# Mean and 1/std of three chunks sent round through DRAM, with their columns on partitions from the start, in a fused long-convolution and Mish-MLP kernel

## The chip, the cores and the metric

The kernel runs on one core of a Trainium2 chip. The metric is the device time of one execution in microseconds (us).

## The reference

The input q has 2048 rows of 448 columns. The kernel adds three things: q itself, a gated long convolution, and an MLP. Both branches work on the layer-normed q.

```python
x = A_q
xn = _layernorm(x, axis=-1)          # (x - mean) / sqrt(var + 1e-5), without scale and shift
return x + _A_ref(xn, A_k, A_v, A_shift_k, A_ssm_k, A_ssm_D) + _B_ref(xn, B_w1, B_b1, B_w2)
# _A_ref: kv = (causal conv of k with 4 taps) * v
#         y  = causal conv of kv with a 2048-long filter per column (by FFT) + kv * D;   result xn * y
# _B_ref: h  = xn @ w1 + b1  (448 -> 1792);  act = h * tanh(softplus(h));   result act @ w2  (1792 -> 448)
```

## The kernel before

**Layout.** The 2048 rows form 8 chunks of 256 rows. A chunk is two row groups `jj` of 128 rows with rows on partitions. The layout is [128 partitions, 16 groups, 448 columns].

**The MLP on TensorE (PE).** Each chunk has seven pairs `p` of 256 hidden units, so there are 56 pairs. Numbers are split into a high part (fp32r) and a rest (fp32r), and products are summed from three parts. A pair has a first product (`g1_mm`, L437, 22 matmuls with the columns of q on partitions: `XH`, `XL`), Mish on ScalarE (ACT; `mish`, L445), a split of the result (`ach` by ACT, `acl` by VectorE (DVE), L73 and L74), and two pairs later a second product (`g2_mm`, L462 to L464, 12 matmuls).

**The layer norm.** `ln_load` fetches the chunk's rows, `Q[c]`. `ln_parts` holds the steps: statistics on DVE (L369 to L375, ending in `ve` = var + eps), 1/std by a power on GpSimd (POOL, L378), the normed rows `xn` on POOL for chunks 1 to 6 and on DVE for chunks 0 and 7 (L382), and a copy of the last 64 columns (L386). The first product wants columns on partitions. So `ln_T` puts four PE transposes per row group (L397) into a PSUM buffer of the first product, ACT casts them to `XH` (L409) and DVE subtracts to get `XL` (L407). Mean and 1/std also serve the gate at the end, in `mv` and `rstd`.

**The convolution** has four steps and uses PSUM buffers of its own, two `pc` of two banks. First, transforms of 8 groups of the filter and of kv (`f1_mm`, L124) go to DRAM, `Dh` and `Dkv`. Then there are eight octets of frequencies: loads `ah` and `av`, a pass over H and a pass over V (`f2_mm`, L198), which ACT copies out as `hs` and `vs`, products on DVE (`prod`, L231: `ya`, `yb`, `yc`, `yd`) and an inverse pass (`i1_mm`, L241), whose result `qe` goes to `E` in DRAM. The last step loads `E` by chunk (`e_load`, L274, two halves `jj` of 64 partitions, both from POOL's queue), folds it on DVE (L280, L282), multiplies (`i2_mm`, L300) and gates (`gate`, L313 and L315).

**The outputs.** For chunks 0 to 5 the MLP's sum goes to DRAM as `ACC` and comes back for the gate: `qa_load` fetches q and ACC into one of three buffers, and `gate_out` sends the result out, all on SyncE's queue (SP). Chunks 6 and 7 stay in SBUF until the end; their MLP sums are added by `g2_evac` (L469), which also sends them out.

**The order** is set by hand. Each pair is two half steps: the even one holds the first product, the odd one Mish and the second product of the pair two back. `at(t, ...)` puts work ahead of half step t, `after(t, ...)` behind it. `H0_AT` and `OCT_AT` place the octets, `I2_AT` the four groups of two chunks of the last step. Small DVE operations wait in the list `drip` and are taken one by one by `dv()` between others; `dv(len(drip))` empties it. Every engine works its own list in order, and so does each DMA queue.

Of the kernel before, what the change touches and what calls it, by code (L numbers as in the profile page):

```python
# [7 lines left out]
F32 = mybir.dt.float32  # L8
# [9 lines left out]
NP = NF // 2  # L18
# [6 lines left out]
H_HEAD = 1  # L25
H_AT = {2: 4, 3: 8, 0: 12, 4: 16, 5: 20, 6: 26, 7: 32}
KV_AT = (24, 29, 34, 39, 44, 50, 55, 60)
H0_AT = 63
OCT_AT = (65, 3)
I2_AT = {98: (6, 7), 102: (0, 1), 106: (2, 3), 111: (4, 5)}  # L30
LATE = 2
WARM = 4
WARM_N = 448


@with_exitstack
def tile_kernel(ctx: ExitStack, tc, q, k, v, sk, hT, sD, w1, b1, w2, c_f1, c_g, c_gi, c_i2, out):
    nc = tc.nc
    V = nc.vector

# [14 lines left out]
    Dkv = dp.tile([NO * 16, 32, D], F32, name="Dkv")  # L55
    E = dp.tile([64, NJ * 4, D], F32, name="E")
    ACC = dp.tile([128, NJ, D], F32, name="ACC")

    f1id = cp.tile([128, 2, 128], F32, name="f1id")
    f1, ident = f1id[:, 0], f1id[:, 1]  # L60
# [11 lines left out]
    def split(h, l, raw):  # L72
        nc.scalar.copy(h, raw)  # L73
        V.tensor_sub(l, raw, h)  # L74
# [7 lines left out]
    def dv(n=1):  # L82
        for _ in range(n):
            if drip:
                drip.pop(0)()
# [183 lines left out]
    def e_load(c):  # L269

        e = EE[c] = t3([128, 2, 2, D], "e3", 4)
        src = E.rearrange("(h k) (m j b) d -> j k m h b d", h=2, m=2, b=2)
        for jj in range(2):
            nc.gpsimd.dma_start(e[64 * jj:64 * jj + 64].rearrange("p h b d -> p h (b d)"),  # L274
                              src[2 * c + jj].rearrange("k m h b d -> (k m) h (b d)"))

    def fold(c):
# [70 lines left out]
        split(w2h[:, 2 * p:2 * p + 2], w2l[:, 2 * p:2 * p + 2], RW.pop(("2", p)))  # L348


    XS, XN = {}, {}

    def ln_load(c, eng=None):
        Q[c] = mp.tile([128, 2, D], F32, name="qt", tag="qt", bufs=3)
        if c:
            nc.sync.dma_start(Q[c], q[:, 2 * c:2 * c + 2])
        else:
            for jj in range(2):
                nc.sync.dma_start(Q[c][:, jj], q[:, jj])

    def ln_parts(c):
        st = mp.tile([128, 2, 6], F32, name="bst", bufs=2)
        ve = mp.tile([128, 2], F32, name="ve", bufs=2)
        xn = mp.tile([128, 2, D + 64], F32, name="xn", tag="xn", bufs=1)
        XN[c] = xn
        eng = nc.gpsimd if 0 < c < NCHUNK - 1 else V

        def stats(jj):
            V.bn_stats(st[:, jj], Q[c][:, jj])  # L369

        def aggr(jj):
            V.bn_aggr(mv[:, 2 * c + jj], st[:, jj])

        def eps(a, b):
            V.tensor_scalar(ve[:, a:b], mv[:, 2 * c + a:2 * c + b, 1], EPS, None, op0=ALU.add)  # L375

        def power(a, b):
            nc.gpsimd.tensor_tensor(rstd[:, 2 * c + a:2 * c + b], ve[:, a:b], mhalf[:, a:b], op=ALU.pow)  # L378

        def norm(jj):  # L380
            j = 2 * c + jj
            eng.tensor_scalar(xn[:, jj, :D], Q[c][:, jj], mv[:, j, 0:1], rstd[:, j:j + 1],  # L382
                              op0=ALU.subtract, op1=ALU.mult)

        def tail(a, b):
            eng.tensor_copy(xn[:, a:b, D:], xn[:, a:b, D - 64:D])  # L386

        return stats, aggr, eps, power, norm, tail

    def ln_stats(c):  # L390
        stats, aggr, eps, power, norm, tail = ln_parts(c)
        drip.extend([lambda: stats(0), lambda: stats(1), lambda: aggr(0), lambda: aggr(1), lambda: eps(0, 2),
                     lambda: [f(*a) for f, *a in ((power, 0, 2), (norm, 0), (norm, 1), (tail, 0, 2))]])

    def transposes(c, jj, p):
        for kt in range(4):
# [79 lines left out]
    def mlp_slot(s):  # L476
        i, half = divmod(s, 2)
        n = len(pairs)
        j = i - G2_LAG
        if half == 0:  # L480
            if i < n:
                c, p = pairs[i]
                if c + 1 < NCHUNK:
                    if p == 0:
                        ln_load(c + 1)
                    if p == (2 if c else 3):
                        ln_stats(c + 1)
                    if c == 0:
                        dv(len(drip))
                    if p == NP - 1:  # L490
                        ln_T(c + 1, 1)
                g1_mm(i)
        else:
            if i < n:
                c, p = pairs[i]
                if p == NP - 2 and c + 1 < NCHUNK:
                    ln_T(c + 1, 0)
                mish(i)
            if 0 <= j < n - 1:
# [179 lines left out]
```

## Time and profile before

| | |
|---|---|
| time, median of 3 runs (lowest, highest) | 378.37 us (377.31, 380.5) |
| the profiled execution's own time | 377.21 us |
| its span, first to last instruction | 375.3 us |
| granted clock of PE, mean | 0.996 |
| DMA | 82.11 MB, mean 219 GB/s |

In rows of engine work a timeline gives start (us from the span's start), duration, engine, line and operation with output and inputs, and in brackets the idle time before it with what ended it. A row of a group (lines) gives the count, busy us in all, mean ns of one, then the engine's idle time before them. PEld is PE's weight load, which overlaps the matmuls; a matmul's row lasts longer than its distance to the next, since matmuls are pipelined, so what one costs PE is read from start to start. A row of DMA issues gives KB of one and the median us from issue to landing.

### The profile page before, as it was taken

The numbers are of one execution on the slowest core, as the hardware profiler recorded it, in microseconds if no ns is written. First come the engines' busy times: TensorE is split into PE (matmuls) and PEld (weight loads), VectorE is DVE, ScalarE is ACT, GpSimd is POOL, SyncE is SP. The second block draws the span as 40 slices with busy tenths as digits, with TensorE's granted clock in tenths as the row PEclk, the third lists the DMA queues.
The fourth block names the chain that finished last, engine by engine and source line by source line (L and its number), as shares of the span: only waits on it lengthen the run. The fifth ranks groups of instructions, "written<-read, shape, count | busy, mean of one in ns | idle before, by whom it ended". The sixth has DMA issues, their size and how long they took to land.

```text
span 375.3 us, 7470 instructions
## 1 busy us (share of the span) xinstructions
PE 364.6 (97%) x3128; PEld 293.0 (78%) x3128; DVE 277.2 (74%) x370; ACT 158.7 (42%) x265; POOL 52.3 (14%) x49
## 2 busy tenths in 40 slices
PE   8999999999999999999999999999999999999994
PEld 2788888878888988988886666666666799688973
DVE  3899748999999999996534746744754915799593
ACT  2785642434424423333433755554755243213210
POOL 2107000700051003300023000140000005220000
PEclk9999999999999999999999999999999999999998
DMA  8899968749488427604885587868480778999466
GB/s 307 308 308 342 388 227 236 205 109 284 121 279 239 100 51 246 196 3 103 255 264 184 207 273 244 274 221 277 153 296 33 253 291 190 224 190 274 155 192 249
DMA packets 32564, 82.11 MB, mean 219 GB/s; under 512 B 2962, under 2 KB 18195, under 8 KB 32531
## 3 DMA queue, kind: packets, MB, share of 16 engines
q1 hardware_dynamic: 22130, 51.69, 41.4%
q10 hardware_dynamic: 9120, 22.61, 20.1%
q0 software_dynamic: 1280, 7.34, 8.7%
q8 instruction: 24, 0.39, 0.4%
q14 instruction: 10, 0.07, 0.1%
HBM read 53.19 MB, written 28.44 MB: 218 GB/s over the span
## 4 chain that ended last, share of the span: by engine, by line
PE 63%; DMA 14%; DVE 13%; issue 4%; ACT 4%; POOL 1%; ACTq 0%; DVEq 0%; SPq 0%; POOLq 0%
PE pg L437 26%; PE pg L462 8%; PE pg L463 7%; PE pg L464 7%; PE pc L198 7%; DMA out_dram<-q 4%; PE pc L124 3%; PE pc L241 3%; DMA a<-ACC 3%; DMA e<-E 2%; ACT a L445 2%; DMA Dkv<-st 1%; PE pg L397 1%; DMA av<-Dkv 1%; DVE acl L74 1%
## 5 line engine op out<-in xcount | busy, mean ns | idle before, releaser
L445 ACT ACTIVATE a<-pg,b1t 128x256 f32<-128x256 f32 x112 | 47.0, 472 | 119.7 <-PE pg L437 101.2
L437 PE MATMUL pg<-XH,w1h 128*128 128x256 f32 x448 | 91.1, 285 | 1.2 <-ACT XH L409 0.7
L437 PEld LDWEIGHTS pg<-XH,w1h 128*128 128x128 f32 x448 | 69.6, 188 | 18.1 <-issue 15.7
L462 PE MATMUL pg<-w2h,ach 128*128 128x448 f32 x224 | 83.3, 372 | 0.2 <-DVE qt L469 0.2
L463 PE MATMUL pg<-w2l,ach 128*128 128x448 f32 x224 | 81.4, 363 | 0.6 <-DVE w2l L74 0.6
L464 PE MATMUL pg<-w2h,acl 128*128 128x448 f32 x224 | 81.4, 363 | 0.0
L74 DVE TENSOR_TENSOR acl<-a,ach 128x512 fp32r<-128x512 f32 x56 | 38.4, 686 | 47.9 <-ACT ach L73 47.7
L437 PE MATMUL pg<-XL,w1h 128*128 128x256 f32 x448 | 69.6, 277 | 0.0
L437 PEld LDWEIGHTS pg<-XL,w1h 128*128 128x128 f32 x448 | 59.4, 188 | 0.1
L437 PE MATMUL pg<-XH,w1l 128*128 128x256 f32 x336 | 56.8, 278 | 0.0
L462 PEld LDWEIGHTS pg<-w2h,ach 128*128 128x128 f32 x224 | 42.0, 187 | 12.7 <-issue 10.4
L437 PEld LDWEIGHTS pg<-XH,w1l 128*128 128x128 f32 x336 | 46.8, 188 | 0.1
L463 PEld LDWEIGHTS pg<-w2l,ach 128*128 128x128 f32 x224 | 42.1, 188 | 3.5 <-DVE w2l L74 1.1
L378 POOL TENSOR_TENSOR rstd<-ve,mhalf 128x2 f32<-128x2 f32 (+1 forms) x9 | 8.5, 944 | 258.6 <-DVE ve L375 220.3
L464 PEld LDWEIGHTS pg<-w2h,acl 128*128 128x128 f32 x224 | 42.1, 188 | 2.6
L73 ACT CAST ach<-a 128x512 fp32r<-128x512 f32 x56 | 34.7, 620 | 1.8
L382 POOL TENSOR_SCALAR xn<-qt,mv,rstd 128x448 f32<-128x448 f32 x12 | 28.3, 2361 | 0.6
L162 DVE TENSOR_TENSOR x<-x 128x896 f32<-128x896 f32 x24 | 26.7, 1113 | 0.8
L409 ACT CAST XH<-pg 128x512 fp32r<-128x512 f32 x16 | 9.4, 587 | 36.9 <-PE pg L397 36.7
L407 DVE TENSOR_TENSOR XL<-pg,XH 128x512 fp32r<-128x512 f32 x16 | 10.9, 686 | 13.7 <-ACT XH L409 13.5
L130 ACT COPY st<-pc 128x896 f32<-128x896 f32 x16 | 14.5, 909 | 15.3 <-PE pc L124 13.2
L131 DVE TENSOR_TENSOR st<-pc,st 128x896 f32<-128x896 f32 x16 | 17.4, 1087 | 3.4 <-ACT st L130 3.1
(63 smaller groups left out, 393.3 us busy)
## 6 DMA issues: line engine op xcount, KB each, us to landing
Dh<-st ACTq DMA_DIRECT2D x16, 448.0 KB, 5.4
Dkv<-st ACTq DMA_DIRECT2D x16, 448.0 KB, 5.2
ah<-Dh SPq DMA_DIRECT2D x8, 896.0 KB, 5.2
av<-Dkv SPq DMA_DIRECT2D x8, 896.0 KB, 4.9
E<-qe ACTq DMA_DIRECT2D x8, 896.0 KB, 4.6
e<-E POOLq DMA_DIRECT2D x16, 448.0 KB, 10.0
kr<-in_k_dram SPq DMA_DIRECT2D x10, 448.0 KB, 6.6
kr<-in_w_dram SPq DMA_DIRECT2D x7, 512.0 KB, 6.4
```

What stands on the lines that cost most here:

```text
L73: nc.scalar.copy(h, raw)
L74: V.tensor_sub(l, raw, h)
L130: nc.scalar.copy(st[:, 1], o)
L131: V.tensor_add(st[:, 0], e, st[:, 1])
L162: V.tensor_add(KV[g], KV[g], o)
L198: nc.tensor.matmul(p[32 * t:32 * t + 32, r, :D], g[rs, t, c], a[rs, t], start=True, stop=True, tile_position=(64 * r, 32 * t))
L382: eng.tensor_scalar(xn[:, jj, :D], Q[c][:, jj], mv[:, j, 0:1], rstd[:, j:j + 1], op0=ALU.subtract, op1=ALU.mult)
L437: nc.tensor.matmul(ps[:, n], l, r, start=n_ == 0, stop=n_ == len(mm) - 1)
L445: nc.scalar.activation(a[:, n], ps[:, n], AF.Mish, bias=b1t[:, 2 * p + n:2 * p + n + 1])
L462: nc.tensor.matmul(ps, ah[:, n, cs], w2h[:, f], start=f == 0, stop=False)
L463: nc.tensor.matmul(ps, ah[:, n, cs], w2l[:, f], start=False, stop=False)
L464: nc.tensor.matmul(ps, al[:, n, cs], w2h[:, f], start=False, stop=f == NF - 1)
```

## The change

For chunks 5 to 7 (`QT_FROM` = 5) a further input `qT` holds q's rows with columns on partitions, cut into three blocks [128, 4, 256]; the fourth 128 columns are the last 64 twice, as with the copy in the kernel before. `qT_load` fetches a block into the tile `xn`. `ln_out` writes the chunk's means and 1/std, 256 numbers each, to the DRAM tile `MR` (values of 4 bytes, two per partition), and `ln_back` reads those 512 numbers into all 128 partitions, both on POOL's queue. `ln_apply` puts four passes on DVE, two that subtract and two that multiply; `x_both` casts `XH` on ACT and subtracts `XL` on DVE. The chunk's transposes, its normed rows on POOL or DVE and their copy fall away. `Q[c]` is still loaded, for the statistics and the sums; its three buffers are now named, and the broadcast lands in the one that is free at that time.

The octets and their first H pass stand one half step later, and three of the four groups of the last step too; the last group stays. The second half `jj` of the slabs of the first group (chunks 6 and 7) is loaded from SP's queue.

```diff
-H0_AT = 63
-OCT_AT = (65, 3)
-I2_AT = {98: (6, 7), 102: (0, 1), 106: (2, 3), 111: (4, 5)}
+H0_AT = 64
+OCT_AT = (66,3)
+I2_AT = {99: (6, 7), 103: (0, 1), 107: (2, 3), 111: (4, 5)}
 LATE = 2
+QT_FROM = 5
...
+    MR = dp.tile([NCHUNK, 2, 2, 128], F32, name="MR")
...
         for jj in range(2):
-            nc.gpsimd.dma_start(e[64 * jj:64 * jj + 64].rearrange("p h b d -> p h (b d)"),
+            (nc.sync if jj and c in I2_AT[min(I2_AT)] else nc.gpsimd).dma_start(e[64 * jj:64 * jj + 64].rearrange("p h b d -> p h (b d)"),
...
-    XS, XN = {}, {}
+    XS, XN, MB = {}, {}, {}
+    QB = [mp.tile([128, 2, D], F32, name="qt%d" % n, bufs=1) for n in range(3)]
 
     def ln_load(c, eng=None):
-        Q[c] = mp.tile([128, 2, D], F32, name="qt", tag="qt", bufs=3)
+        Q[c] = QB[c % 3]
...
-        xn = mp.tile([128, 2, D + 64], F32, name="xn", tag="xn", bufs=1)
-        XN[c] = xn
-        eng = nc.gpsimd if 0 < c < NCHUNK - 1 else V
+        if c < QT_FROM:
+            XN[c] = xn = mp.tile([128, 2, D + 64], F32, name="xn", tag="xn", bufs=1)
+        eng = nc.gpsimd if c else V
...
-                     lambda: [f(*a) for f, *a in ((power, 0, 2), (norm, 0), (norm, 1), (tail, 0, 2))]])
+                     lambda: [f(*a) for f, *a in ((power, 0, 2),) + (((norm, 0), (norm, 1), (tail, 0, 2)) if c < QT_FROM else ())]])
+
+    def ln_out(c):
+        for w, t in enumerate((mv[:, 2 * c:2 * c + 2, 0], rstd[:, 2 * c:2 * c + 2])):
+            nc.gpsimd.dma_start(MR[c, w].rearrange("j p -> p j"), t)
+
+    def ln_back(c):
+        MB[c] = QB[(c + 1) % 3].rearrange("p a b -> p (a b)")[:, :2 * CH].rearrange("p (a b) -> p a b", a=2)
+        nc.gpsimd.dma_start(MB[c], MR[c].rearrange("w j p -> (w j p)").partition_broadcast(128))
+
+    def qT_load(c):
+        XN[c] = mp.tile([128, 4, CH], F32, name="xn", tag="xn", bufs=1)
+        nc.sync.dma_start(XN[c], qT[c - QT_FROM])
+
+    def ln_apply(c):
+        x, mb = XN[c], MB.pop(c)
+        for op, w in ((V.tensor_sub, 0), (V.tensor_mul, 1)):
+            for kt in range(0, 4, 2):
+                drip.append(lambda op=op, w=w, kt=kt: op(x[:, kt:kt + 2], x[:, kt:kt + 2], mb[:, w:w + 1].to_broadcast([128, 2, CH])))
+
+    def x_both(c):
+        dv(len(drip))
+        x_tiles(c)
+        split(*XS[c], XN.pop(c))
...
-                    if p == NP - 1:
+                    if p == NP - 1 and c + 1 < QT_FROM:
                         ln_T(c + 1, 1)
...
-                if p == NP - 2 and c + 1 < NCHUNK:
+                if p == NP - 2 and c + 1 < QT_FROM:
                     ln_T(c + 1, 0)
...
+    for c in range(QT_FROM, NCHUNK):
+        t = 2 * NP * (c - 1)
+        after(t + 6, lambda: dv(len(drip)))
+        at(t + 7, qT_load, c)
+        at(t + 7, ln_out, c)
+        at(t + 7, ln_back, c)
+        after(t + 8, ln_apply, c)
+        after(t + 10, lambda: dv(len(drip)))
+        after(t + 11, x_both, c)
```

Three places show the new order. The first is PE in the octet stage, ahead of chunk 5's first product, in the kernel before (`ah` and `av` are octet 1's passes; rows of `pg` with `ach` are the second product, with `XH` the first):

```order
L198 MATMUL pc<-ah,g 32x448 x16
L397 MATMUL pg_2265<-f1id,xn 128x128 x4
L462 MATMUL pg_2053<-w2h,ach 128x448
...
L464 MATMUL pg_2057<-w2h,acl 128x448
L198 MATMUL pc<-av,g 32x448 x16
L397 MATMUL pg_2319<-f1id,xn 128x128 x4
L437 MATMUL pg_2326<-XH,w1h 128x256 x3
```

The two rows of transposes (`f1id,xn`) are gone in the change, here and in chunks 6 and 7; nothing takes their place on PE.

The second is chunk 7: POOL from the power to the first slabs of the last step, in the change,

```order
L381 TENSOR_TENSOR rstd<-ve,mhalf 128x2
L401 DMA MR<-mv 128x2x1
L401 DMA MR<-rstd 128x2x1
L406 DMA qt_95<-MR 128x512
L276 DMA e_3489<-E 64x2x896
L276 DMA e_3492<-E 64x2x896
L276 DMA e_3522<-E 64x2x896 x2
```

and DVE from octet 7's products to the folds of the first group, before and then in the change (`yc` and `yd` are products, `z` and below is the gate, not shown):

```order
L375 TENSOR_SCALAR ve<-mv 128x2
L74 TENSOR_TENSOR acl<-a,ach 128x512
L382 TENSOR_SCALAR xn<-qt,mv,rstd 128x448 x2
L386 COPY xn<-xn 128x2x64
L407 TENSOR_TENSOR XL<-pg_3520,XH 128x4x128
L74 TENSOR_TENSOR acl<-a,ach 128x512
L280 TENSOR_TENSOR ex<-e_3479 128x896
L282 TENSOR_TENSOR e_3479<-e_3479 128x896
```

```order
L378 TENSOR_SCALAR ve<-mv 128x2
L233 TENSOR_TENSOR yd<-vs,hs 128x896
L233 TENSOR_TENSOR yc<-yc,yd 128x896
L76 TENSOR_TENSOR acl<-a,ach 128x512 x2
L416 TENSOR_TENSOR xn<-xn,qt_95 128x512 x4
L76 TENSOR_TENSOR acl<-a,ach 128x512
L76 TENSOR_TENSOR XL<-xn,XH 128x1024
L282 TENSOR_TENSOR ex<-e_3489 128x896
L284 TENSOR_TENSOR e_3489<-e_3489 128x896
```

On POOL the two writes of `MR` and the broadcast (into `qt_95`) stand behind the power, and of chunks 6 and 7 (`e_3489`, `e_3492`) one half each is left. On DVE `ve` stands ahead of the last products instead of behind them, and two products and two `acl` lie between it and the passes over `xn`.

The third is PE at the second group of the last step (`pc<-ex` and `pc<-e`), before and then in the change:

```order
L464 MATMUL pg_3348<-w2h,acl 128x448
L300 MATMUL pc<-ex,i_3450 32x448 x2
...
L437 MATMUL pg_3751<-XH,w1h 128x256 x3
...
L462 MATMUL pg_3795<-w2h,ach 128x448
```

```order
L492 MATMUL pg_3326<-w2h,acl 128x448
L465 MATMUL pg_3708<-XH,w1h 128x256 x3
...
L302 MATMUL pc<-ex,i_3457 32x448 x2
...
L490 MATMUL pg_3756<-w2h,ach 128x448
```

The group stands behind the first product of that pair instead of ahead of it. On SP, the q and ACC loads of the second and third chunk of the last step now stand behind the two `e` halves.

More of the change, by code (lines that the diff above doesn't have):

```diff
@@ L36, in tile_kernel @@
 @with_exitstack
-def tile_kernel(ctx: ExitStack, tc, q, k, v, sk, hT, sD, w1, b1, w2, c_f1, c_g, c_gi, c_i2, out):
+def tile_kernel(ctx: ExitStack, tc, q, qT, k, v, sk, hT, sD, w1, b1, w2, c_f1, c_g, c_gi, c_i2, out):
     nc = tc.nc
@@ L660 @@
     lay = lambda x: x.reshape(32, 2, 2, 16, D).transpose(2, 1, 0, 3, 4).reshape(128, NJ, D)
+    qT = lay(a["A_q"][0])[:, 2 * QT_FROM:].transpose(2, 1, 0)
+    qT = np.concatenate([qT, qT[384:]]).reshape(4, 128, NCHUNK - QT_FROM, CH).transpose(2, 1, 0, 3)
     kpad = np.pad(a["A_k"][0], ((4, 0), (0, 0)))
     arrs = dict(
-        q=lay(a["A_q"][0]), k=np.concatenate([lay(kpad[:S])[:, :, :][:, :4], lay(a["A_k"][0])], axis=1),
+        q=lay(a["A_q"][0]), qT=qT, k=np.concatenate([lay(kpad[:S])[:, :, :][:, :4], lay(a["A_k"][0])], axis=1),
         v=lay(a["A_v"][0]), sk=a["A_shift_k"].T, hT=lay(a["A_ssm_k"].T), sD=a["A_ssm_D"][None],
```

## Prediction

> **What bounds the kernel now.** I read the busy times first, then the stages, the waits, and last the chain that ended last. The first row is from the page; the others are the table by stage (window, length, busy time of each engine, granted clock, DMA share, GB/s).
>
> ```profile
> PE 364.6 (97%) x3128; PEld 293.0 (78%) x3128; DVE 277.2 (74%) x370; ACT 158.7 (42%) x265; POOL 52.3 (14%) x49
> 178.40:292.50 114.10, 112.92 (x1222) 79.31 (x1221) 64.02 (x76) 60.82 (x92) 11.62 (x8) 1.00 0.68 220
> 320.70:334.10 13.40, 12.78 (x101) 9.90 (x100) 12.82 (x17) 2.92 (x6) 2.34 (x4) 1.00 1.02 225
> 334.10:370.10 36.00, 35.98 (x291) 29.99 (x290) 28.88 (x41) 7.30 (x15) 2.33 (x4) 1.00 0.75 215
> ```
>
> PE is busy at full clock from the start to 370.1. In the octet stage (178 to 292) DVE works 64 us of 114, so there it has room; from 320.7 on it has little. What PE still loses shows in the waits (us in total, times, longest):
>
> ```profile
> PEld pc L300 <- DVE e L282: 1.8, 2, 1.0
> PEld pc L300 <- DVE ex L280: 1.2, 1, 1.2
> PEld pc L198 <- ACT hs L209: 1.5, 2, 0.8
> PEld pc L241 <- DVE yc L231: 1.2, 1, 1.2
> PE pc L198 <- DMA av<-Dkv: 0.3, 1, 0.3
> ```
>
> Small, but of the size of what is at stake. The chain in order of time (start, us, what) tells what sets the very end, and the last matmul stands below it:
>
> ```profile
> 338.96 9.42 DMA out_dram<-q
> 348.79 5.90 DMA a<-ACC
> 356.77 6.11 DMA out_dram<-q
> 363.28 4.94 DMA a<-ACC
> 368.31 0.69 DVE q L315
> 370.85 0.53 DVE qt L469
> ```
> ```profile
> 369.72 0.36 PE L464 MATMUL pg<-w2h,acl 128*128 128x448 f32 x1
> ```
>
> The tail is not PE. Chunks 0 to 5 share three gate buffers, so each load of q and ACC for the next chunk waits on SP's queue until an earlier chunk's out slab has landed. This string starts with chunk 0's gate and ends with chunk 5's; DVE evacuates the last sums only behind it, at 370.85. PE's last matmul ends at 370.08, so PE alone could end some 0.7 us earlier and no more.
>
> **Transposes.** The octet stage shows one chunk's pair (chunk 5):
>
> ```profile
> 200.60 0.66 PE L397 MATMUL pg<-f1id,xn 128*128 128x128 f32 x4
> 201.01 0.45 PE L462 MATMUL pg<-w2h,ach 128*128 128x448 f32 x1
> 204.13 1.79 PE L198 MATMUL pc<-av,g 64*32 64x448 f32 x32 [0.46 <-ACT hs L209]
> 205.85 0.66 PE L397 MATMUL pg<-f1id,xn 128*128 128x128 f32 x4
> 206.26 0.60 PE L437 MATMUL pg<-XH,w1h 128*128 128x256 f32 x3
> ```
>
> Four transposes hold PE from 200.60 to 201.01, 0.41 us by starts; six such groups go: **-2.4**. Their first half also queues an XH cast on ACT ahead of the hs copies, so the V pass at 204.13 waited 0.46; the same shape stands in chunk 6. In the change one XH cast from SBUF needs no PE result and stands ahead of hs only if xn is late: **-0.9** (bounds 0 and the 1.5 of the wait row).
>
> **The round trip that replaces them.** Per chunk: POOL's power, two MR issues, one broadcast issue, two landings in a row; then four subtract or multiply passes of 128x512 on DVE, one XH cast and one XL of 128x1024.
>
> ```profile
> L378 POOL TENSOR_TENSOR rstd<-ve,mhalf 128x2 f32<-128x2 f32 x7 | 7.3, 1046 | 253.2 <-DVE ve L375 220.3 <-DMA x<-in_v_dram 32.9
> L274 POOL DMA_DIRECT2D e<-E x16 | 9.6, 608 | 22.5 <-DVE acl L74 9.8 <-DVE ex L280 7.6 <-ACT ach L73 3.8
> DMA to landing us min/median/max: 5.0/10.0/15.2
> i<-in_c_i_dram SPq DMA_DIRECT2D x1, 32.0 KB, 2.4
> L74 DVE TENSOR_TENSOR acl<-a,ach 128x512 fp32r<-128x512 f32 x56 | 38.4, 686 | 47.9 <-ACT ach L73 47.7
> L330 ACT CAST w1h<-kr 128x1024 fp32r<-128x1024 f32 x6 | 6.3, 1047 | 1.1 <-DMA kr<-in_w_dram 1.1
> L209 ACT COPY hs<-pc 128x896 f32<-128x896 f32 x16 | 13.7, 909 | 3.7 <-PE pc L198 3.7
> 182.21 0.17 DVE L372 BATCH_NORM_AGGREGATE mv<-bst 128x2 f32<-128x6 f32 x1
> 209.01 1.69 PE pc L241 x32
> ```
>
> (The third row is the landing time of the e slabs, POOL's only DMAs.) Power and three issues are 1.05 + 3 x 0.61 = 2.9 us. No row shows a transfer like MR's, 256 values of 4 bytes. Below, a landing is bounded by the 32 KB constant, 2.4; above, by the quickest e slab, 5.0, since MR is far smaller and the broadcast is 256 KB against 448. Middle 3.7: 2.9 + 7.4 = **10.3 us** (7.7 to 12.9). With the e slabs' median of 10.0, eight of them queued, it is 22.9.
>
> What covers it: in chunk 7, `ve` is forced after half step 90, and chunk 7's first matmul stands in half step 98. Between lie an estimated 1.4 of half step 90, octet 7's inverse pass of 1.69, and seven products of 2.5 (first and second products; rows 299.85 to 302.46 and 318.16 to 320.66 below): 20.6 us. DVE and ACT then need 4 x 0.69 for the passes (an estimate from acl, the same size), 0.69 for an acl, 1.05 for XH and some 1.2 for XL, 5.6 in all: **15.0** are left. In chunk 5 `ve` moves up to some 182.7, behind the row at 182.21. The first that can suffer is the V pass of octet 1 in half step 69, which needs ACT's two hs copies behind XH. Until then lie 2.2 of half step 62, six products of 2.5 and three passes of 1.7, 22.3; less 2.7 for the passes, 1.05 for XH and 1.8 for hs, 16.7. So the trip is hidden with 2 us or more to spare, and so are the 2.5 us that DVE works more per chunk, in a stage where it is 56% busy. If the trip is late, acl and the octet's products queue behind the waiting passes on DVE, hs behind XH on ACT, and PE waits for those. I allow **+0.4** for small waits (bounds 0 and the third rival).
>
> The Trainium skill, "DMA: Bandwidth & Descriptors" (Rules for kernel authors), says that a non-contiguous last dimension lowers to one descriptor per element, which MR's write is. By the Trainium skill's same page (Anatomy of one DMA) a GpSimd DMA has about 2.0 us fixed, and the trip would be an estimated 7 us; the trace's e slabs never landed under 5.0. No run here shows what 256 single elements cost.
>
> **The later half steps.** Octets start half a step later, with the same spacing; this moves work and adds none. Waits at the edges (0.3 for av; the inverse pass of octet 7 broke for yc) had too little lead, and the change gives av 2.5 us more and puts `ve` of chunk 7 among the products: **-0.7** of some 1.0 (bounds 0 and 1.0).
>
> The last step's four groups stand at half steps 99, 103, 107, 111 instead of 98, 102, 106, 111.
>
> ```profile
> 299.85 0.62 PE L437 MATMUL pg<-XH,w1h 128*128 128x256 f32 x3
> 302.46 0.36 PE L462 MATMUL pg<-w2h,ach 128*128 128x448 f32 x1
> 318.16 0.37 PE L462 MATMUL pg<-w2h,ach 128*128 128x448 f32 x1
> 320.66 0.57 PE L300 MATMUL pc<-ex,i 64*32 64x448 f32 x2
> 324.10 0.62 PE L437 MATMUL pg<-XH,w1h 128*128 128x256 f32 x3
> 334.13 0.57 PE L300 MATMUL pc<-ex,i 64*32 64x448 f32 x2
> 335.80 0.62 PE L437 MATMUL pg<-XH,w1h 128*128 128x256 f32 x3
> ```
>
> The second group feeds chunk 0's gate and starts the string of the tail. It now stands behind one more first product, 302.46 - 299.85: **+2.6**. From its start, 334.13, to the span's end are 41.2 us, and this distance stays, since it is made of landings. So the end moves by all that PE gains ahead of the second group, less 2.6; what PE gains behind it is worth 0.7 at most.
>
> The first group took 320.66 to 324.10, 3.44 us; the second, unhindered, 1.67. The 1.8 between were spent on chunk 7's e slab:
>
> ```profile
> 309.53 4.90 POOL L274 DMA_DIRECT2D e<-E  x8 [3.77 <-ACT ach L73]
> 320.93 1.09 DVE L280 TENSOR_TENSOR ex<-e 128x896 f32<-128x896 f32 x1 [1.87 <-DMA e<-E]
> q0 software_dynamic: 536, 3.15, 89.7%
> ```
>
> Its halves were third and fourth of the eight that POOL issued from 309.53 on; now they are second on POOL and second on SP. They are issued once E has landed. That last E write went out beside six prefetches of q and ACC; four of these now stand behind SP's e halves and so cannot slow it. I take the wait as gone: **-1.8**. Bounds: gone, or 2 us longer, if POOL's next slabs (3.15 MB in 16 us, so 2.3 us each) slip in between.
>
> Chunk 6's out slabs, which shared their time with the four e slabs at 335, go out ahead of the second group now. The first landing of the string, 9.42 against 6.11 for a later one, can shorten: **-0.6** (bounds 0 and the 2.7 at which PE, with 36.0 - 2.6 us left, sets the end).
>
> **Sum.** -2.4 - 0.9 + 0.4 - 0.7 + 2.6 - 1.8 - 0.6 = -3.4. The profiled execution took 377.21 with a span of 375.3; 371.9 of span give **373.8 us**. The median of the runs shown is 378.37, 1.2 above the profiled one, so this is 1.2% under the median. Differences under 1% can't be told from none in this kernel; the line for faster is 374.6.
>
> **Rivals.** *The last step keeps its wait* (25%). For: POOL's queue alone held the 16 DMA engines 89.7% busy in those 16 us (last row above), so a second queue may bring e no sooner. Then the -1.8 is missing, 375.6, up to 377.7 with the longer bound. Against: the four prefetches are out of the way and E lands earlier. The Trainium skill, "DMA: Bandwidth & Descriptors" (Issuing engines are not separate DMA queues), states this rule: transfers started on several engines run on the same 16 DMA engines and interleave, and only issue time is saved; by that, the trace's 89.7% agrees.
>
> *The tail shortens until PE sets it* (13%). Chunk 6's outs are gone and the string loses 2.7 instead of 0.6: 371.7. Against: the e slabs still run there, DMA share 0.75.
>
> *The round trip is late* (13%), the case on the other side. For: its transfers wait for one another, beside octet loads at a DMA share of 0.68, and the e row's median is 10.0. Lateness is 2.9 + 2L - 15.0 in chunk 7 and 2.9 + 2L - 16.7 in chunk 5, L being one landing. From L = 7.3 it eats the 3.4, from 8.6 the kernel is over 1% slower; at 10.0 it loses 7.9 + 6.2 = 14.1, which gives 387.9. Against: the quickest e slab took 5.0 and is larger; 10.0 belongs to a queue of eight. The Trainium skill's rule of one descriptor per element, named above, speaks for this case.
>
> **How the numbers follow.** My forecast, 373.8, has 49%; its own terms spread it from 371.5 to 375.6, about 0.35 of it under 374.6. Faster: 0.35 + 0.13 + 0.03 from the first rival = 0.51. Slower: most of the late trip, 0.12. Same: the remaining 0.37. The range leaves out the worst late trips and the best tails: 370.8 to 379.0.
>
> **What would show it.** Right: 40 transposes instead of 64; no wait of PE on xn, MR or the qt tile that holds the broadcast; passes on xn starting when acl frees DVE, not when the broadcast lands; the second group near 331 and chunk 0's out slab near 336; the first group at about 1.7 us. Wrong: DVE idle ahead of xn for over 3 us with the broadcast as its releaser, hs or XH as releasers of PE in the octet stage, chunk 7's e landing after PE's slot, or a tail longer than 41 us from the second group.

## The result, and the profile after

| | before | after |
|---|---|---|
| time, median (lowest, highest), 6 runs each | 378.12 us (377.31, 382.13) | 396.17 us (393.67, 397.79) |
| ratio, 95% interval | | 1.0493 (1.0458 to 1.0528) |
| the profiled execution's own time | 377.21 us | 395.33 us |
| its span | 375.3 us | 393.5 us |
| granted clock of PE, mean | 0.996 | 0.987 |

The change makes the kernel 4.9% slower. The span grew by 18.2 us. I had forecast 3.4 us less.

The busy times, and three stretches of the table by stage (window, length, busy time of PE, PEld, DVE, ACT and POOL, granted clock, DMA share, GB/s):

```profile
PE 369.9 (94%) x3104; PEld 292.4 (74%) x3104; DVE 282.8 (72%) x376; ACT 159.1 (40%) x262; POOL 47.2 (12%) x50
181.90:217.50 35.60, 30.59 (x297) 21.82 (x295) 13.39 (x20) 13.76 (x21) 2.93 (x4) 0.95 0.62 206
317.00:340.00 23.00, 17.29 (x112) 11.97 (x111) 12.04 (x16) 8.17 (x15) 6.55 (x11) 0.93 0.81 201
340.00:381.00 41.00, 37.14 (x294) 29.19 (x292) 31.30 (x42) 8.76 (x18) 2.38 (x4) 0.96 0.87 231
```

The 24 transposes are gone from PE's count (3128 to 3104). But where PE was busy throughout before, it now stands idle for 5.0 us of the 35.6 around chunk 5, for 5.7 us of the 23 between 317 and 340, where the last step begins, and for 3.9 us of the tail. In these three stretches the mean granted clock is also lower (0.95, 0.93, 0.96): at the end of each of three stops of PE (5.0 us up to 198.8, 4.2 up to 332.4, 3.3 up to 376.9) begin 3.4 us at a clock of 0.5. The waits name who kept whom (us in total, times, longest):

```profile
POOL qt L406 <- DMA MR<-mv: 21.6, 2, 11.0
DVE xn L416 <- DMA qt<-MR: 10.6, 2, 8.2
ACT qe L251 <- DMA E<-qe: 9.7, 1, 9.7
DVE ex L282 <- DMA e<-E: 8.7, 3, 5.0
PE pc L200 <- DMA av<-Dkv: 5.0, 1, 5.0
PE pc L302 <- DVE ex L282: 4.6, 3, 3.3
```

POOL waits for the two writes of MR before it may issue the broadcast, and DVE waits for the broadcast. Two other rows name transfers that the change didn't touch: an av load and an E write. The timeline of chunk 5's trip, on POOL and on DVE:

```profile
183.03 0.95 POOL L401 DMA_DIRECT2D MR<-mv  x1
183.99 0.74 POOL L401 DMA_DIRECT2D MR<-rstd  x1
195.77 0.58 POOL L406 DMA_DIRECT2D qt<-MR  x1 [11.04 <-DMA MR<-mv]
...
201.84 2.49 DVE L416 TENSOR_TENSOR xn<-xn,qt 128x512 f32<-128x512 f32 x4 [8.23 <-DMA qt<-MR]
```

From the first write's issue to the first pass lie 18.8 us. The issues and landings around it, for 180 to 200 us, tell both stories: first after, then the two rows of before that answer to it. The row GB/s has 40 slices of half a microsecond; a row of issues ends with the median us to landing.

```profile
GB/s 149 198 273 247 262 366 394 432 424 409 419 423 392 223 81 0 0 0 0 0 0 0 0 0 0 18 47 82 32 7 54 283 401 409 406 390 402 387 387 384
...
Dkv<-st ACTq DMA_DIRECT2D x2, 448.0 KB, 10.5
av<-Dkv SPq DMA_DIRECT2D x1, 896.0 KB, 6.8
...
qt<-MR POOLq DMA_DIRECT2D x1, 256.0 KB, 6.0
...
MR<-mv POOLq DMA_DIRECT2D x1, 1.0 KB, 12.0
MR<-rstd POOLq DMA_DIRECT2D x1, 1.0 KB, 11.2
```
```profile
av<-Dkv SPq DMA_DIRECT2D x2, 896.0 KB, 4.9
Dkv<-st ACTq DMA_DIRECT2D x2, 448.0 KB, 5.3
```

A write of 1 KB takes 12.0 us. While the two are under way the data rate is zero for 5 us (187.5 to 192.5), although a Dkv write issued before them hasn't landed: it takes 10.5 us, where such a write took 5.3. The av load reads Dkv, so it is issued late (at 191.9), and the V pass of octet 0 waits for it: PE stands for 5.0 us up to 198.8, and the pass then takes 3.2 us, 1.5 more than the H pass before it, at the clock of 0.5. At chunk 7 it is a write of E that lands late. These rows give us to landing of the eight E writes (lowest, median, highest), after and then before:

```profile
DMA to landing us min/median/max: 3.9/5.7/16.9
```
```profile
DMA to landing us min/median/max: 3.8/4.6/7.1
```

The write of 16.9 us, issued at 299.74, holds its buffer; ACT's next copy `qe` waits 9.7 us for it, so the last E write goes out at 318.5 instead of 301.7. Not all of the 16.9 us can be MR's doing: chunk 7's MR writes were issued only from 305.6 on, and eleven of this E write's sixteen completion counts had come by 307.4, late already against the 4.6 us of before; the other five came from 312.0 to 316.7, the MR writes landing at 316.9 and 317.1. With PE's broadcast in place of MR (below) the same write, beside the same prefetches, takes 8.1 us. Behind that comes the chain to the end (start, us, what):

```profile
327.37 20.77 DMA e<-E
355.37 12.58 DMA out_dram<-q
368.35 5.27 DMA a<-ACC
375.66 5.38 DMA out_dram<-q
381.48 4.90 DMA a<-ACC
388.47 0.53 DVE qt L497
```

The second group starts at 348.23 and chunk 0's out slab takes 12.58 us instead of 9.42, and the slabs are among the links.

**Where the 18.2 us lie.** Four landings in the trace cut the end of the program into pieces: the last E write, the last of the sixteen e slabs, chunk 0's out slab, the span's end (us; the differences in brackets).

| | E lands | last slab | chunk 0's out slab | end of span |
|---|---|---|---|---|
| before | 308.8 | 347.3 (38.5) | 348.4 (1.1) | 375.3 (26.9) |
| after | 323.6 | 367.4 (43.8) | 368.0 (0.5) | 393.5 (25.5) |

So E lands 14.9 us later, the slabs take 5.3 us more, and the rest takes 1.9 us less. The experiments ask for the cause of the first two.

### The profile page after: what moved, and what is told of

Read it like the earlier page. It is cut to its first block, busy times and chain, and to the rows that moved or that the text cites. A ratio compares the mean times of both kernels' runs of the same rounds, so it can differ in the third digit from the quotient of the medians.

```text
span 393.5 us, 7451 instructions
## 1 busy us (share of the span) xinstructions
PE 369.9 (94%) x3104; PEld 292.4 (74%) x3104; DVE 282.8 (72%) x376; ACT 159.1 (40%) x262; POOL 47.2 (12%) x50
## 5 line engine op out<-in xcount | busy, mean ns | idle before, releaser
L381 POOL TENSOR_TENSOR rstd<-ve,mhalf 128x2 f32<-128x2 f32 (+1 forms) x9 | 7.6, 845 | 242.5 <-DVE ve L378 238.3
L302 PE MATMUL pc<-ex,i 64*32 64x448 f32 x64 | 13.4, 658 | 8.7 <-DVE ex L282 4.6
L251 ACT COPY qe<-pc 128x896 f32<-128x896 f32 x16 | 13.8, 911 | 19.3 <-DMA E<-qe 9.7
L200 PE MATMUL pc<-av,g 64*32 64x448 f32 x256 | 16.6, 591 | 5.1 <-DMA av<-Dkv 5.0
L220 ACT COPY vs<-pc 128x896 f32<-128x896 f32 x16 | 13.8, 909 | 17.8 <-PE pc L200 16.1
```

The source lines that it names most:

```text
L200: nc.tensor.matmul(p[32 * t:32 * t + 32, r, :D], g[rs, t, c], a[rs, t], start=True, stop=True, tile_position=(64 * r, 32 * t))
L220: nc.scalar.copy(PV[o][:, c], p[:, :, :D])
L251: nc.scalar.copy(qe[:, 2 * i:2 * i + 2], p[:, :, :D])
```

## The experiments

**My theory after the result:** the writes of single 4-byte values into the same 2 KB of DRAM land slowly, and transfers of other parts that are under way land late with them; the waits on both make the loss. **Rivals:** the new half steps and SP's e halves are to blame; or the trip is merely too long for its cover, as the third rival of the prediction had it, and nothing else is disturbed. Ratios are to the kernel before on the same chip, with a 95% interval.

**The two parts apart.** First the half steps and SP's halves alone, with the transposes kept; then the layout and the trip alone.

```diff
 # the kernel before
-H0_AT = 63
-OCT_AT = (65, 3)
-I2_AT = {98: (6, 7), 102: (0, 1), 106: (2, 3), 111: (4, 5)}
+H0_AT = 64
+OCT_AT = (66,3)
+I2_AT = {99: (6, 7), 103: (0, 1), 107: (2, 3), 111: (4, 5)}
...
-            nc.gpsimd.dma_start(e[64 * jj:64 * jj + 64].rearrange("p h b d -> p h (b d)"),
+            (nc.sync if jj and c in I2_AT[min(I2_AT)] else nc.gpsimd).dma_start(e[64 * jj:64 * jj + 64].rearrange("p h b d -> p h (b d)"),
```

> The kernel before with the later half steps and the SP halves of the first slabs, transposes kept. Theory (the 4-byte writes of MR are the loss): 377.6, by the forecast's own terms +2.6 - 1.8 - 0.7 - 0.6, within 375 to 381. Rival (the later half steps and the SP halves are the loss): 388 or more, most of the 18 us.

> The change without the later half steps and with all slabs on POOL's queue. Theory (MR's writes): still slow, 391 to 400, each MR write landing 10 us or more after its issue. Rival (the later half steps): 374 to 378.

The half steps alone: 378.37 us, 1.0029 (0.9998 to 1.0059). The trip alone, with the half steps and POOL's slabs of before: 403.54 us, 1.0669 (1.0587 to 1.0752). That is more than the 391 to 400 expected. The whole loss sits in the trip, and the later half steps with SP's halves even ease it. The waits of the trip alone say how:

```profile
DVE xn L416 <- DMA qt<-MR: 28.1, 3, 13.4
PE pc L243 <- ACT vs L220: 10.7, 1, 10.7
```

The passes over `xn` wait 28.1 us for the broadcast instead of 10.6, and here they do hold up PE, by way of ACT's copy `vs`, which waits for an octet's product behind them on DVE: 10.7 us. In the change this wait of PE's is 0.2 us.

**The writes alone.** The kernel before, transposes and all, with the two MR writes added for chunks 5 to 7 and nobody reading them; `ve` is forced earlier as in the change. Beside it the same without the writes, and one that gives each value 512 bytes of its own.

```diff
 # the kernel before, and this
+    def ln_out(c):
+        for w, t in enumerate((mv[:, 2 * c:2 * c + 2, 0], rstd[:, 2 * c:2 * c + 2])):
+            nc.gpsimd.dma_start(MR[c, w].rearrange("j p -> p j"), t)
...
+        after(t + 6, lambda: dv(len(drip)))
+        at(t + 7, ln_out, c)
```
```diff
 # 512 bytes for each value
-    MR = dp.tile([NCHUNK, 2, 2, 128], F32, name="MR")
+    MR = dp.tile([NCHUNK, 2, 2, 128, 128], F32, name="MR")
...
-            nc.gpsimd.dma_start(MR[c, w].rearrange("j p -> p j"), t)
+            nc.gpsimd.dma_start(MR[c, w, :, :, 0].rearrange("j p -> p j"), t)
```

> The kernel before plus the two MR writes of chunks 5 to 7 (ve forced at the same half step), which nothing reads; transposes kept, no broadcast. Theory (the writes hold up other transfers that are under way, above all Dkv and E): 384 to 392, with an E write beside them landing after 9 us or more in place of 4.6. Rival (only the passes that wait for the trip lose time): 378, no change.

> The control for the writes alone: the kernel before with only ve of chunks 5 to 7 forced at the earlier half step, no writes. Theory (all of the loss of that run is the writes): 377, no change. Rival (the earlier ve and the norm that goes with it displace DVE and POOL work): 380 to 386.

> The run with the writes alone, but each of the 512 values of a chunk goes to an address of its own 512 bytes from the next; nothing reads them. If what costs is that many small writes meet in the same 2 KB of DRAM: landings of 3 to 5 us and a time within 1% of before. If each piece costs wherever it goes: landings of 9 us or more and about 386 as before.

The writes alone: 386.21 us, 1.0227 (1.0159 to 1.0296), though no instruction waits for them. Without them 376.07 us, 1.0005 (0.9977 to 1.0034). With 512 bytes for each value 377.05 us, 1.0021 (0.9994 to 1.0048). The landings of MR (lowest, median, highest; of the crowded six only four are on record), crowded and then spread:

```profile
DMA to landing us min/median/max: 11.5/12.4/12.9
```
```profile
DMA to landing us min/median/max: 2.3/5.7/6.4
```

And those of the eight E writes in the same two kernels:

```profile
DMA to landing us min/median/max: 3.8/4.0/13.4
```
```profile
DMA to landing us min/median/max: 3.8/3.9/7.4
```

As many pieces of the same size land in half the time if each has its own 512 bytes, and the loss is gone. So the piece itself isn't what costs; the crowding is. The last E write, issued just behind the crowded MR writes of chunk 7, takes 13.4 us instead of 7.4, so E lands at 318.7; without the writes it lands at 308.5. The Trainium skill's "DMA: Bandwidth & Descriptors" (Rules for kernel authors) has one descriptor per element for such a write, which both of these kernels share, so that rule alone doesn't tell them apart. The Trainium skill's same page (Specifications) says that below 512 B the DMA engine reads, modifies and writes back; writes into the same stretch would then have to follow one another, and the landings of MR above agree with that. That it is this mechanism no run here shows.

**Whose queue.** The same writes from SP's queue instead of POOL's:

```diff
-            nc.gpsimd.dma_start(MR[c, w].rearrange("j p -> p j"), t)
+            nc.sync.dma_start(MR[c, w].rearrange("j p -> p j"), t)
```

> The kernel before with the two unread writes of 256 values of 4 bytes for chunks 5 to 7, as in the run with the writes alone, but from SP's queue instead of POOL's. Theory (the crowding of small writes in the same 2 KB of DRAM is slow, whoever issues them): they land after 9 to 13 us again, E writes or loads beside them take 9 us or more, span 382 to 387. Rival (POOL's queue is what is slow): they land in 3 to 6 us and the span is 374 to 377.

From a single run: span 392.7 us, time 394.52. MR's landings in it:

```profile
DMA to landing us min/median/max: 8.9/9.8/10.4
```

They are slow from SP too. The rival falls. The span is longer than the 382 to 387 expected; that kernel's last E write landed only at 325.9. Why that run lost more than the one from POOL's queue stays open.

**The trip cured: rows of 16 bytes.** POOL packs the two means and two 1/std of a partition into one row, and one write sends 128 rows of 16 bytes; DVE reads the broadcast with a stride.

```diff
 # the change
-    MR = dp.tile([NCHUNK, 2, 2, 128], F32, name="MR")
+    MR = dp.tile([NCHUNK, 128, 4], F32, name="MR")
...
-        for w, t in enumerate((mv[:, 2 * c:2 * c + 2, 0], rstd[:, 2 * c:2 * c + 2])):
-            nc.gpsimd.dma_start(MR[c, w].rearrange("j p -> p j"), t)
+        r = mp.tile([128, 4], F32, name="mr4", bufs=2)
+        nc.gpsimd.tensor_copy(r[:, 0:2], mv[:, 2 * c:2 * c + 2, 0])
+        nc.gpsimd.tensor_copy(r[:, 2:4], rstd[:, 2 * c:2 * c + 2])
+        nc.gpsimd.dma_start(MR[c], r)
...
```

> The change with mean and 1/std of a row put side by side on POOL, written to MR as 128 rows of 16 bytes instead of 512 single values, and read back as one piece; DVE's passes read it with a stride. Theory, if the time of a write goes with the number of its pieces: one landing near 4 us in place of 11 and 372 to 378. If a small write costs the same whatever their number: 393 to 398. Rival (the later half steps are the loss): 393 to 398 with a short landing.

378.77 us, 1.0038 (1.0000 to 1.0077). Landings of MR and broadcast together in this kernel:

```profile
DMA to landing us min/median/max: 2.3/5.4/6.1
```

These 128 rows, too, lie side by side in 2 KB and land fast: what was slow is 256 single values to a write, crowded, and not small neighbouring pieces as such. The second group starts at 331.91, where the prediction wanted it ("near 331"). The loss of 18 us is gone, and yet the kernel isn't faster than before; its 378.77 lies just above the 372 to 378 expected. The cure was then tried with POOL's queue for all slabs, and once more with the half steps of before as well:

> The rows of 16 bytes with the new half steps, but all slabs of the last step on POOL's queue again. Theory (the SP halves let the q and ACC loads of two chunks fall in among the e slabs, which lengthens the tail from the second group from 41.2 to 44 us): a tail of 41 to 42 us and 374 to 377. If the SP halves earn their place by ending the first group's wait: 378 to 381.

> The change with mean and 1/std sent as 128 rows of 16 bytes, and with the octets, the groups of the last step and the slabs' queue as in the kernel before. Theory (a trip that lands in 2 to 6 us is hidden, and the new layout then saves PE 2.4 to 3.3 us): PE reaches the second group at 331 to 332.5 and the time is 374 to 375.5, ratio 0.990 to 0.995. Rival (the trip's transfers still hold up E, as its first group waited 5.5 us in the run with the new times and POOL's slabs): the first group waits 3 us or more, second group at 334 or later, time 377 or more.

New half steps with POOL's slabs: 376.52 us, 1.0008 (0.9978 to 1.0038). The time is in the range, but not for the reason given: the first group waits 5.5 us, the second starts only at 336.6, and the tail behind it is 38.7 us, not 41 to 42. Old half steps: 383.48 us, 1.0190 (1.0152 to 1.0228). I had expected the latter to be the fastest; it fails. Its waits:

```profile
ACT vs L220 <- DVE yd L233: 9.0, 2, 7.2
DVE xn L419 <- DMA qt<-MR: 7.7, 3, 3.7
```

The passes over `xn` wait for a broadcast that is 3.7 us late, the octet's products queue behind them on DVE, and ACT waits 7.2 us for the last product before it may write `vs`. So a trip with two landings of some 5 us is all but covered with the new half steps (`xn` waits 2.1 us once) and not with those of before: in this version the later half steps are what hides it. This is the chain of waits that the prediction named for a late trip.

**The trip cured: no DRAM at all.** Four PE products with the identity spread a chunk's means and 1/std over a PSUM buffer, and ACT copies it into the free buffer.

```diff
 # the change
     def ln_back(c):
+        ps = g1p.tile([128, 2, CH], F32, name="pg1")
+        for w in range(2):
+            for jj in range(2):
+                s = rstd[:, 2 * c + jj:2 * c + jj + 1] if w else mv[:, 2 * c + jj, 0:1]
+                nc.tensor.matmul(ps[:, w, 128 * jj:128 * jj + 128], s.to_broadcast([128, 128]), ident, start=True, stop=True)
...
-        nc.gpsimd.dma_start(MB[c], MR[c].rearrange("w j p -> (w j p)").partition_broadcast(128))
+        nc.scalar.copy(MB[c], ps)
...
-        at(t + 7, ln_out, c)
-        at(t + 7, ln_back, c)
+        at(t + 8, ln_back, c)
```

> The change with mean and 1/std brought to all partitions by four PE matmuls per chunk (the value as weights, repeated over 128 columns, times the identity) and one ACT copy, instead of the way through DRAM; the new times and the SP halves kept. Theory (with no MR the loss is gone; the SP halves still cost the tail some 3 us): 376 to 380. If the new times were the loss: over 390.

> The change with its new layout for chunks 5 to 7, but with the 256 means and 256 1/std of a chunk spread by four small PE products and an ACT copy instead of DRAM, and with the octets, the groups of the last step and the slabs' queue as in the kernel before. Theory (the slow trip and what it held up were the whole loss, and the new layout saves PE little): the six groups of transposes (2.4 us) are paid back by six pairs of small products (0.9 us a chunk in the run with the new times, 2.7 us), so the time is that of the kernel before within 1%: 376 (374.5 to 378), second group near 333.5. Rival (the half steps are what ate the gain, +2.6 and the longer tail): without them the time falls to 373.5 to 374.5, 1% or more under the kernel before.

With the new half steps 377.37 us, 1.0013 (0.9987 to 1.0040); with those of before 377.36 us, 1.0032 (1.0006 to 1.0058). In the first, chunk 5's broadcast on PE:

```profile
186.31 0.61 PE L403 MATMUL pg<-f1id,mv 128*128 128x128 f32 x4
186.76 0.61 PE L403 MATMUL pg<-f1id,rstd 128*128 128x128 f32 x4
187.30 1.74 PE L199 MATMUL pc<-ah,g 64*32 64x448 f32 x32
```

From 186.31 to 187.30 are 1.0 us a chunk, which pays back the 2.4 us of the transposes. The theory stated for the second kernel held in the time (its second group came at 334.9, not near 333.5): taking back the half steps, together with SP's halves, gains nothing.

**Where does the rest of the gain go?** In the kernel with PE's broadcast and new half steps no trip is left, the first group has no wait, and the second group starts at 331.97, 2.2 us earlier than before. Still the span is 375.4. Its landings, in the columns of the table above, are 305.8, 349.6 (43.9), 350.1 (0.5), 375.4 (25.3): E lands 3.0 us earlier, and the slabs take 5.4 us longer. New theory: chunk 0's out slab lands when the last e slab has, whenever the second group starts; and the gate loads of chunks 1 and 2, which now stand behind SP's e halves, run among the slabs. The rival is the prediction's own assumption, a fixed distance from the second group to the end.

First a version that puts these loads ahead of SP's halves again and moves the second and third group back by half a step:

```diff
 # the change with PE's broadcast
-I2_AT = {99: (6, 7), 103: (0, 1), 107: (2, 3), 111: (4, 5)}
+I2_AT = {99: (6, 7), 102: (0, 1), 106: (2, 3), 111: (4, 5)}
...
-            at(ts[n - 1] + (2 if m else -2 if n == 2 else -1) if n > 1 else ts[0] - 5 + m, qa_load, c)
+            at(ts[0] - 5 if c < 3 else ts[n - 1] + (2 if m else -1) if n > 1 else ts[0] - 5 + m, qa_load, c)
```

> The change with PE's broadcast, the octets half a step later, the second and third groups of the last step back at half steps 102 and 106, SP's halves kept, and the first three loads of q and ACC put ahead of SP's halves. Theory (the half step costs 2.6 at the second group, and the tail is longer only because gate loads queue behind SP's halves and run among the slabs): second group at 329 to 330, first out slab of the gate lands in about 9 us as before, tail 41, span 371 to 372.5, time 373 to 374.5. Rival (the slabs need SP's queue clear of gate loads, so E comes later): first group waits 3 us or more, second group 332 or later, time 376 or more.

375.44 us, 0.9962 (0.9934 to 0.9990): 0.4% under the kernel before, by an interval that barely leaves 1 out, and the lowest ratio of many full versions; so a real gain isn't shown. And the span is 374.5 and the first group waited 2.0 us, between theory and rival. The loads now run beside octet 6's E write, and the chain shows it:

```profile
293.54 11.64 DMA E<-qe
...
349.53 6.30 DMA out_dram<-q
```

An E write of 11.64 us makes the last one late: E lands at 311.2, the last slab 36.2 us later. What is gained on one side is lost on the other.

Next, the loads from ACT's queue behind the last E write, with the second group at half step 103 and then at 102:

```diff
 # the change with PE's broadcast
-            nc.sync.dma_start(qt, q[:, 2 * c:2 * c + 2])
-            nc.sync.dma_start(ac, ACC[:, 2 * c:2 * c + 2])
+            eng = nc.scalar if c in (1, 2) else nc.sync
+            eng.dma_start(qt, q[:, 2 * c:2 * c + 2])
+            eng.dma_start(ac, ACC[:, 2 * c:2 * c + 2])
...
-            at(ts[n - 1] + (2 if m else -2 if n == 2 else -1) if n > 1 else ts[0] - 5 + m, qa_load, c)
+            at(ts[0] - 5 if c < 3 else ts[n - 1] + (2 if m else -2 if n == 2 else -1) if n > 1 else ts[0] - 5 + m, qa_load, c)
```

> The change with PE's broadcast and the new times, as before, but the q and ACC loads of chunks 1 and 2 go out from ACT's queue right behind the last E write, instead of from SP's queue behind its two e halves. Theory (chunk 0's out slab lands when the last of the sixteen slabs has, so the end hangs on when E lands and on how many bytes run between that and the last slab, not on the second group): the four loads run in the 4 to 5 us before the first slab's data flow, the last slab lands at 344 to 346 instead of 349.6 and chunk 0's out slab right behind it, span 371 to 373, time 373 to 375, while the second group stays at 332. Rival (the string starts with the second group and keeps its distance of 43.4 us): the span stays at 375 to 376 whatever these loads do.

> The same with the second and third groups of the last step half a step earlier (102 and 106 instead of 103 and 107). Theory (the slabs set the end, the groups only follow): the second group starts 2 to 2.6 us earlier, 329.5 to 330, and the time stays within 1 us of the run with 103 and 107. Rival (the second group's start sets the end): the time falls by 2 to 2.6 us against that run.

376.87 us, 0.9999 (0.9975 to 1.0023), and 377.49 us, 1.0017 (0.9994 to 1.0041). The first missed its aim: the loads went out at 306.9 and later, beside the slabs again, and the last slab landed at 349.1, so its forecast of 373 to 375 fell. The second is the telling one: its second group starts 3.6 us earlier (329.52 against 333.15), and the end doesn't come earlier (375.3 against 374.5). Its rival, 2 to 2.6 us less, falls.

Last, the bytes alone: half of each of the four loads taken away, and as many bytes added as copies within DRAM.

```diff
 # the change with PE's broadcast: half
+            nj = 1 if c in (1, 2) else 2
-            nc.sync.dma_start(qt, q[:, 2 * c:2 * c + 2])
-            nc.sync.dma_start(ac, ACC[:, 2 * c:2 * c + 2])
+            nc.sync.dma_start(qt[:, :nj], q[:, 2 * c:2 * c + nj])
+            nc.sync.dma_start(ac[:, :nj], ACC[:, 2 * c:2 * c + nj])
...
```
```diff
 # the change with PE's broadcast: more
             nc.sync.dma_start(ac, ACC[:, 2 * c:2 * c + 2])
+            if c in (1, 2):
+                nc.sync.dma_start(MORE[:, 4 * c - 4:4 * c - 2], q[:, 2 * c:2 * c + 2])
```

> The change with PE's broadcast and the new times, with only half of each of the four q and ACC loads of chunks 1 and 2 that SP's queue carries behind the e halves (0.92 MB less of transfers; it leaves out the second row groups of chunks 1 and 2, whose gate takes the first ones' rows instead). Theory (the end hangs on the bytes between E's landing and the last slab): at the slabs' 224 GB/s that is 4.1 us less, the last slab lands near 345.5 instead of 349.6, chunk 0's out slab near 346.5, and the span falls from 375.4 to 371 to 372.5. Rival (the second group sets the start of the string): span 375 to 376, chunk 0's out slab lands at 350 again.

> The same kernel with full loads and 0.92 MB more: behind the loads of chunks 1 and 2 SP's queue also copies 448 KB of q each within DRAM, unread. Theory: 4.1 us more, the last slab at 353 to 354, chunk 0's out slab near 354.7, span 379 to 380.5. Rival (the second group): span 375 to 376.

Half: 374.28 us, 0.9924 (0.9898 to 0.9950), span 372.4. Its second group starts at 332.69, 0.7 us later than with full loads, and its string is early nevertheless:

```profile
337.96 9.28 DMA out_dram<-q
```

More: 379.32 us, 1.0052 (1.0024 to 1.0080), span 376.4. All landings of this question in one table (us from the traces; slabs counts from E's landing):

| kernel | second group | E lands | last slab (slabs) | chunk 0's out slab | end |
|---|---|---|---|---|---|
| before | 334.1 | 308.8 | 347.3 (38.5) | 348.4 | 375.3 |
| half steps and SP's halves alone | 336.5 | 309.5 | 353.0 (43.5) | 352.8 | 377.6 |
| 16 bytes, new half steps | 331.9 | 307.6 | 349.2 (41.6) | 350.2 | 376.1 |
| the same, POOL's slabs | 336.6 | 310.6 | 349.8 (39.3) | 350.4 | 375.3 |
| PE's broadcast, new half steps | 332.0 | 305.8 | 349.6 (43.9) | 350.1 | 375.4 |
| loads from ACT, group at 103 | 333.2 | 306.2 | 349.1 (42.9) | 350.2 | 374.5 |
| loads from ACT, group at 102 | 329.5 | 305.3 | 347.5 (42.2) | 348.5 | 375.3 |
| half of the loads | 332.7 | 307.1 | 347.1 (40.0) | 347.3 | 372.4 |
| 0.92 MB more in DRAM | 331.8 | 305.7 | 349.6 (43.8) | 351.0 | 376.4 |

Chunk 0's out slab lands within 1.4 us of the last slab in every row, while its distance to the second group runs from 13.8 to 19.2 us. From the last slab to the end there are still 24.6 to 28.0 us; why this differs from kernel to kernel stays open. Taking 0.92 MB of loads away shortens the slabs by 3.8 us; 4.1 were expected. Since E landed 1.3 us later there, the last slab came 2.5 us earlier. Adding 0.92 MB within DRAM, under way beside the slabs from 308.4 to 344.7, didn't lengthen them in the trace, which the theory had wrong by 4.1 us: it isn't any byte that counts, but the loads that go into SBUF beside the slabs. That trace is of an execution of 378.15 us, though, 1.2 under this kernel's median, so a smaller cost of the copies isn't ruled out. Which resource these two share and the copies within DRAM don't, stays open.

## Why the prediction was wrong, point by point

**The round trip, +0.4: the step that failed.** The prediction bounded a landing "above, by the quickest e slab, 5.0, since MR is far smaller". Size was the wrong measure. The MR writes landed after 10.8 to 12.0 us (four of the six are on record), the broadcast after 3.7 to 7.0. Then the third rival's sum gives, in chunk 7, 2.9 + 11.3 + 3.7 - 15.0 = 2.9 us of lateness, and in chunk 5, 2.9 + 12.0 + 6.0 - 16.7 = 4.2 (chunk 7's cover is 14.9 by its own terms, which add up to 5.7 and not 5.6; that changes nothing). That is 7 us, not 18: it was the nearest rival, but its price named only those who wait for the trip. In the change these didn't hold PE up: in the octet stage PE waited for an av load, and for neither hs nor XH.

**What no case had: transfers that the change doesn't touch land late.** The writes with no reader cost 2.3% by themselves. In the change this made the av load and the E write late, and with E the whole last step: E landed 17.9 us later than in the kernel with PE's broadcast and otherwise the same order. The two traces split the 17.9: octet 1's H pass starts 6.3 us later (207.2 against 200.9), behind PE's wait at chunk 5; the seventh E write goes out 7.7 us later (299.7 against 292.0) and the last one 16.6 (318.5 against 301.9), the 8.9 between being ACT's wait for the seventh (9.7 against 0.8); the last write itself takes 1.3 us more. That seventh write, with the prefetches beside it, takes 8.1 us even without MR, against 3.9 in the kernel before, so these parts are not MR's alone.

**The transposes, -2.4, and the waits, -0.9 and -0.7: borne out.** With the trip cured by rows of 16 bytes the second group started at 331.9. From before's 334.1, the terms -2.4, -0.9, -0.7, +2.6 and the 0.9 that the first group's wait shortened there make 331.8. Four waits of PE in the octet stage before, for hs (0.5), qe (0.5), yc (0.4) and av (0.3), some 1.6 us together, are gone in it. The sum fits; no run measured the transposes' 2.4 by itself.

**The first group's wait, -1.8: right once the trip is cured.** With SP's halves and the loads behind them it waited not at all (PE's broadcast) or 0.9 us (16 bytes); with POOL's queue alone 5.5 us (16 bytes) and 3.6 us (PE's broadcast, old half steps). The first rival falls.

**"This distance stays, since it is made of landings": failed, and with it "tail -0.6".** The prediction moved four prefetches out of the way of E and took that as free. E did land 3.0 us earlier, and the same loads then ran among the slabs, 5.4 us. The string of the tail starts with the landing of the last slab, not with the second group's start. So the 2 us that PE won there were worth nothing, and the +2.6 of the half step was weighed at the wrong place too: with PE's broadcast the kernel takes the same time with the new order (half steps and SP's halves) and with the old one. Without its trip's damage the change comes out even (1.0013 with PE's broadcast, 1.0038 with rows of 16 bytes), not 1.2% faster; even the layout alone, with PE's broadcast at the old times, wins nothing.

**The list of what would show it** worked: it named DVE idle ahead of xn with the broadcast as releaser (8.2 us), e landing late (5.0), and a tail over 41 us (45.3). It had no sign for late landings of transfers that the change leaves alone.

## What to carry to other kernels

Weigh a DMA by how its pieces lie in DRAM, not by its bytes: here 1 KB of single 4-byte values side by side took longer to land (10.8 to 12.0 us) than most writes of 896 KB (3.9 to 6.2), and it held up others that had nothing to do with it. Packing them into rows or broadcasting on PE cured it; spreading them did so for writes that nobody reads. Before giving PE's gain at a late stage a value, find the landing on which the end hangs, and follow every transfer that a reordering moves to the place where it runs instead.

## What the runs showed of the hardware

- 256 values of 4 bytes, written side by side: 11.5 to 12.9 us to landing when nothing read them. In the change, of one such write the first of its sixteen completion counts came after 3.8 us and the last after 12.0. 512 bytes apart: 2.3 to 6.4 us. As 128 rows of 16 bytes side by side: 2.3 to 5.5 us.
- While two such writes were under way, the data rate was zero for 5 us with another write of 448 KB pending, and that write took 10.5 us instead of 5.3.
- With such writes unread, an E write of 896 KB issued just behind them took 13.4 us; it took 7.4 with the same values 512 bytes apart.
- From POOL's queue or SP's, they were slow alike (11.5 to 12.9 and 8.9 to 10.4 us).
- 0.92 MB copied within DRAM beside the slabs didn't delay them (43.8 us against 43.9); 0.92 MB less of loads into SBUF shortened them by 3.8 us.
- At the end of each of PE's stops of 5.0, 4.2 and 3.3 us in the change, the granted clock went to 0.5 for 3.4 us. The V pass of octet 0 took 3.2 us in one such stretch; the H pass before it took 1.7.
